# Top-k attention into a SwiGLU block: scores and V of two units in every second turn

## The chip, the cores and the metric

The kernel runs on one core of one Trainium2 chip. Its engines run side by side, each with its own in-order queue: TensorE (PE) multiplies matrices into PSUM, VectorE (DVE) selects, ScalarE (ACT) copies out of PSUM and takes exponentials, GpSimd (POOL) does elementwise work, SyncE (SP) issues most transfers. The metric is the device time of one execution in microseconds: a median of 1810.34 us over 8 runs before the change (1808.96 to 1812.03).

## The reference

```python
B, H, S, D = q.shape              # 8, 8, 576, 64, float32
scores = scale * np.matmul(q, k.transpose(0, 1, 3, 2))
kth = np.partition(scores, -32, axis=-1)[..., -32:-31]
scores = np.where(scores >= kth, scores, -1000000000.0)
scores = scores - np.max(scores, axis=-1, keepdims=True)
attn = np.exp(scores)
attn = attn / (np.sum(attn, axis=-1, keepdims=True) + 1e-09)
x = np.matmul(attn, v).transpose(0, 2, 1, 3).reshape(B * S, H * D)
g = x @ w_gate                    # 512 x 1536
silu = g * (1.0 / (1.0 + np.exp(-g)))
out = silu * (x @ w_val) @ w_out  # 1536 x 512
```

Each query keeps its 32 largest scores of 576. The attention's output, 4608 tokens of 512, goes through a feed-forward block (FFN).

## The kernel before

**Units and turns.** The attention is cut into 160 units, in the order of (batch, query tile, pair of heads): 8 batches, 5 query tiles (four of 128 queries, a last one of 64), 4 pairs of heads. A unit of the first four tiles holds two heads of 128 queries, 1152 columns of scores. A unit of the last tile holds 64 queries of both heads on the 128 partitions, so it counts as one head of 576 columns; a batch ends with four such units. The main loop has a turn n for each unit, and in it several units are worked on at different stages:

- DVE selects for unit n (`select`, L316): four rounds of MAX8 and, between them, MATCH_REPLACE8 on each head, then a mask (L338).
- POOL adds the mask to the scores of unit n-1 (`penalize`, L342). ACT then takes the exponential and its sum (`weigh`, L353), and DVE ends the turn with the reciprocal (L371).
- ACT multiplies by that reciprocal at the start of the next turn (`scaled`, L374), for unit n-2. PE transposes that unit in nine pieces of 128 columns (`turn`, L376), and ACT copies them to `et` (L387).
- PE multiplies V with the transposed weights of unit n-3 (`values`, L391). ACT copies the result to the FFN's input xT (L430).
- PE computes the scores of unit n+1 (`scores`, L278), and ACT copies them to `sc` (L313).
- `fetch` prepares unit n+2: at a batch's first query tile it transposes q and k (`prep`, L248), at the last one it loads q and k of the next batch (`load`, L213).

**Shapes on PE.** The array of 128 rows and 128 columns is used in three shapes. FFN and transposes use all of it. In the scores each of two heads contracts over 64 rows, so two matmuls run side by side in row halves (64*128 in the profile). In V's product each head gives 64 columns, so two run side by side in column halves (128*64). V's last 64 keys of both heads are multiplied at once before the others, on the whole array, with a block-diagonal matrix `vl` of V (L406). The four chunks of other keys follow in column halves (L415). An fp32 matmul is two instructions in the profile.

**The FFN in between.** The FFN goes by blocks of 256 tokens (`feed`, L456), once all four pairs of heads have written their columns of xT. It is a generator: each step, a *piece*, is 8 PE instructions of 256 columns (cost 1) or 6 (cost 0.75, in the second product, which is done with seven half-size products). Two pieces make one gate product or one value product, in one of three PSUM buffers. ACT then works on it: three instructions for a gate (L495 to L497), one copy for a value (L502). These wait in the list `on_act` until `flush(on_act)` is called, at the start of a turn and after the next two pieces, or when `piece` finds two waiting. POOL's products wait in `on_pool` likewise. `share(n)` gives each turn a credit of pieces, about 4.4 for a unit of two heads, from which the cost of the attention's work on PE in that turn is taken.

**Buffers.** Scores, transposes, V's product and the preparation share five PSUM buffers in turn (`ps_t`). `sc` and `e` have three buffers each and `et` two. MATCH_REPLACE8 of unit n+1 writes the `e` buffer that the transposes of unit n-2 read.

**Order.** Every engine but SP executes in the order in which the code issues its instructions: the last lines chain them so. SP's queue is in order too. In turn n PE has V of unit n-3, scores of n+1, two pieces, transposes of n-2, then the other pieces. ACT has what `on_act` holds, `scaled`, the copy to xT, the score copies, `weigh`, `on_act` again, the copies to `et`.

Of the kernel before, what the change touches and what calls it, by code (L numbers as in the profile page):

```python
# [10 lines left out]
FP32 = mybir.dt.float32  # L11
# [4 lines left out]
P = 128  # L16
# [4 lines left out]
BLK = 256  # L21
# [4 lines left out]
def kernel(  # L26
# [37 lines left out]
    nc = tc.nc  # L64
    B, H, S, D = q.shape
    DM, DFF = w_gate.shape
    J = S // P
    JP = J * P
    R = S - JP
    NHP = H // 2  # L70
# [15 lines left out]
    ps_t = ctx.enter_context(tc.tile_pool(name="ps_t", bufs=5, space=PSUM))  # L86
# [6 lines left out]
    for i in range(NV):  # L93
        vt = consts.tile([P, P], FP32, name=f"vlast{i}")
# [135 lines left out]
    vs = {}  # L230

    def load_v(i):
        b, hp = pairs[i]
        h = slice(2 * hp, 2 * hp + 2)
        vt = slabs.tile([P, 2, J, D], FP32, tag="v", name="v")
        v_last = slabs.tile([R, 2, D], FP32, tag="vl", name="v_last")
        vl = vlast[i % NV]
        nc.sync.dma_start(
            vt[:].rearrange("p h j d -> p h (j d)"),
            v[b, h, 0:JP].rearrange("h (p j) d -> p h (j d)", j=J),  # L240
        )
        nc.sync.dma_start(v_last[:], v[b, h, JP:S].rearrange("h p d -> p h d"))
        for hh in range(2):
            o = hh * R
            nc.sync.dma_start(vl[o : o + R, o : o + R], v[b, 2 * hp + hh, JP:S])
        vs[i] = (vt, v_last, vl)
# [24 lines left out]
    units = [(b, qt, hp) for b in range(B) for qt in range(J + 1) for hp in range(NHP)]  # L271
    state = {}

    def n_heads(qt):

        return 1 if qt == J else 2

    def scores(n):  # L278
        b, qt, hp = units[n]
        slab = preps[b * NHP + hp]  # L280
        sc = work.tile([P, 2 * S], FP32, tag="sc", name="sc", bufs=3)
        halves = [slice(0, D), slice(D, P)]
        half = S // 2

        def bank():
            return ps_t.tile([P, 512], FP32, tag="t", name="s")


        if qt == J:
            banks = [bank() for _ in range(2)]  # L290
            for i, ps in enumerate(banks):
                for d in halves:
                    k0 = R + i * half
                    nc.tensor.matmul(  # L294
                        ps[d, 0:half], slab[d, S + R : S + 2 * R], slab[d, k0 : k0 + half]
                    )
            yield
            for i, ps in enumerate(banks):
                nc.scalar.copy(sc[:, i * half : (i + 1) * half], ps[:, 0:half])
        else:  # L300
            q0 = S + 2 * R + qt * P
            banks = []
            for i in range(2):
                for hh, d in enumerate(halves):
                    ps = bank()
                    banks.append((i + 2 * hh, ps))
                    k0 = (1 - hh) * R + i * half
                    nc.tensor.matmul(  # L308
                        ps[:, 0:half], slab[d, q0 : q0 + P], slab[d, k0 : k0 + half]
                    )  # L310
            yield
            for i, ps in banks:
                nc.scalar.copy(sc[:, i * half : (i + 1) * half], ps[:, 0:half])  # L313
        state[n] = dict(sc=sc)
# [38 lines left out]
    def weigh(n):  # L353

        st = state[n]
        e, heads, bias = st["e"], st["heads"], st.pop("bias")
        tot = small.tile([P, 2], FP32, tag="tot", name="tot")
        for t, hs in enumerate(heads):
            nc.scalar.activation(  # L359
                e[:, hs], e[:, hs], AF.Exp, bias=bias[:, t : t + 1], scale=scale,  # L360
                accum_out=tot[:, t : t + 1],
            )
        nh = len(heads)
        nc.scalar.activation(tot[:, 0:nh], tot[:, 0:nh], AF.Identity, bias=eps[:])
        st["tot"] = tot
# [28 lines left out]

    xT, done = {}, {}

    def values(n):

        b, qt, hp = units[n]
        vt, v_last, vl = vs[b * NHP + hp]  # L400
        et = state.pop(n)["et"]
        last = qt == J
        ql = R if last else P
        av = ps_t.tile([P, P], FP32, tag="t", name="av")
        if not last:
            nc.tensor.matmul(av[:], vl[:], et[:, J, :], start=True, stop=False)  # L406
        for c in range(J + 1 if last else J):
            kl = R if c == J else P
            for hh in range(2):
                moving = (  # L410
                    et[0:kl, c, hh * R : (hh + 1) * R]
                    if last
                    else et[:, c + hh * (J + 1), :]
                )
                nc.tensor.matmul(  # L415
                    av[hh * R : (hh + 1) * R, 0:ql],
                    v_last[:, hh, :] if c == J else vt[:, hh, c, :],
                    moving,
                    start=last and c == 0,
                    stop=c == (J if last else J - 1),  # L420
                )
        c0 = b * S + qt * P
        at = c0
        while at < c0 + ql:
            kb = at // BLK
            n_c = min((kb + 1) * BLK, c0 + ql) - at
            if kb not in xT:
                xT[kb] = ffn.tile([P, NHP, BLK], FP32, tag="xT", name="xT", bufs=3)
                done[kb] = 0
            nc.scalar.copy(  # L430
                xT[kb][:, hp, at - kb * BLK : at - kb * BLK + n_c],
                av[:, at - c0 : at - c0 + n_c],
            )
            done[kb] += n_c
            at += n_c

    def store(o, g0, cols=slice(0, DM), queues=(nc.sync,)):
# [14 lines left out]
    def flush(queue):  # L452
        while queue:
            queue.pop(0)()
# [201 lines left out]
    NU = len(units)  # L656
# [22 lines left out]
    def fetch(n):  # L679

        b, qt, hp = units[n]
        i = b * NHP + hp
        if qt == 0:
            yield from prep(i)
        if qt == J and i + NHP < len(pairs):
            load(i + NHP)

    def share(n):


        others = 0.0
        for m, cost in ((n + 1, 0.7), (n - TURN, 0.6), (n - VALUES, 0.7)):
            if m >= 0:
                others += cost * (0.5 if units[m][1] == J else 1)
        if units[n + 2][1] == 0:
            others += 0.6

        beside = 6.4 if T[1] else 7.0
        return beside * n_heads(units[n][1]) / 2 - others

    def pieces(n):
        for _ in range(n):
            if credit[0] >= 1:
                credit[0] -= piece()

    def run(steps):
        for _ in steps:
            pass

    def finish_unit(n):  # L710
        values(n)
        b, qt, hp = units[n]
        if qt == J and b + 1 < B:
            load_v((b + 1) * NHP + hp)

    load(0)
    rounding(2)
# [2 lines left out]
    run(scores(0))  # L720
    early[0]()
    run(fetch(1))
    credit = [0.0]
    no = iter(())
    scaled = no
    TURN, VALUES = 2, 3
    due = [2.0]
    for n in range(NU + VALUES):
        nh = n_heads(units[n][1]) if n < NU else 1
        topk = select(n) if n < NU else no  # L730
        norm = normalize(n - 1) if 0 <= n - 1 < NU else no
        nxt = scores(n + 1) if n + 1 < NU else no
        ahead = fetch(n + 2) if n + 2 < NU else no

        def dve(k, beside=True):

            for _ in range(k * nh):
                next(topk, None)
                due[0] += 5 / 6 if beside else 0
                if due[0] >= 1:  # L740
                    due[0] -= 1
                    rounding(1)

        if n >= NU - NHP:
            credit[0] = 8.0
        else:
            credit[0] = min(credit[0] + share(n), share(n) + 1)
        flush(on_act)
        if 0 <= n - 1 < NU:
            penalize(n - 1)  # L750
        flush(on_pool)
        run(scaled)
        if n >= VALUES:
            finish_unit(n - VALUES)
        run(nxt)
        early[0]()
        if 0 <= n - 1 < NU:
            weigh(n - 1)


        dve(2, beside=False)
        if 2 <= n + 2 < NHP:
            load(n + 2)
        if n < NHP:
            load_v(n)
        pieces(2)
        flush(on_act)
        dve(1)
        dve(1)
        if 0 <= n - TURN < NU:  # L770
            run(turn(n - TURN))

        flush(on_pool)
        next(ahead, None)
        pieces(1)
        next(ahead, None)
        dve(1)
        pieces(1)
        dve(2, beside=False)
        run(topk)  # L780
        next(norm, None)
        scaled = norm
        pieces(6)
# [50 lines left out]
```

## Time and profile before

| | us |
|---|---|
| median of 8 runs | 1810.34 |
| the profiled execution's own time | 1809.62 |
| its span, first to last instruction | 1807.6 |
| PE busy | 1704.9 |
| DVE busy | 1615.5 |
| ACT busy | 1221.8 |
| POOL busy | 1039.9 |

The mean granted clock of PE is 0.963. The profile page divides the span into 40 slices of 45 us, and a digit is an engine's busy share of a slice in tenths. A busy PE in it is not PE at its peak, since matmuls are pipelined: the distance between the starts of two of them is what one costs. A line of waits names who waited and for whom, the total, how many times and the longest. A line of the timeline gives start, length, engine, line of the kernel, operation, output and inputs, shape on the array, sizes and how many instructions were merged.

### The profile page before, as it was taken

How to read it: one execution, taken by the hardware profiler on the slowest of the kernel's cores; microseconds unless marked ns; L12 is line 12 of the kernel's file. 1: busy time of each engine (PE TensorE's matmuls, PEld its weight loads, DVE VectorE, ACT ScalarE, POOL GpSimd, SP SyncE). 2: the span in 40 equal slices, each digit the busy share in tenths (PEclk: the TensorE clock that was granted, in tenths of full speed). 3: DMA queues.
4: the chain of work that ended last, by engine and by line, in shares of the span. 5: the costliest groups of instructions: out<-in, count | busy, mean ns of one | idle time of the engine just before them, and what ended most of it. 6: DMA issues, size and time to landing. Idle time of an engine off the chain costs nothing.

```text
span 1807.6 us, 30379 instructions
## 1 busy us (share of the span) xinstructions
PE 1704.9 (94%) x10756; PEld 1403.4 (78%) x10756; DVE 1615.5 (89%) x3372; ACT 1221.8 (68%) x2977; POOL 1039.9 (58%) x930
## 2 busy tenths in 40 slices
PE   4559999899999999999999999999999999999999
PEld 2437678687888778887888878888888878888877
DVE  7999999999999999998999989998999979999400
ACT  6779676676767676767666676766776667676532
POOL 5778665455564646564555546655556544646434
PEclk6559999899999999999999999999999999999989
DMA  7433030001200030001200021000300011000000
GB/s 191 127 105 94 21 86 1 13 2 45 50 12 3 14 78 5 13 1 29 67 13 1 14 62 32 1 13 4 92 1 13 1 41 28 13 1 13 1 12 12
DMA packets 109304, 59.64 MB, mean 33 GB/s; under 512 B 88544, under 2 KB 96992, under 8 KB 109152
## 3 DMA queue, kind: packets, MB, share of 16 engines
q1 hardware_dynamic: 108016, 57.37, 12.3%
q8 instruction: 85, 1.39, 0.3%
q14 instruction: 67, 0.55, 0.1%
q10 hardware_dynamic: 1136, 0.33, 0.1%
HBM read 48.23 MB, written 9.44 MB: 32 GB/s over the span
## 4 chain that ended last, share of the span: by engine, by line
PE 83%; DVE 7%; ACT 7%; POOL 2%; issue 0%; DMA 0%; SPq 0%; ACTq 0%; POOLq 0%
PE f L470 40%; PE x_ps L556 9%; PE av L415 8%; PE s L308 7%; PE y_ps L556 7%; PE etps L386 6%; DVE m L328 3%; DVE e L332 3%; PE s L294 2%; PE av L406 2%; ACT et L387 1%; PE o_ps L516 1%; ACT e L359 1%; DVE e L338 1%; DVE size L121 1%; ACT kqT L268 1%
## 5 line engine op out<-in xcount | busy, mean ns | idle before, releaser
L328 DVE MAX8 m<-e 128x8 f32<-128x576 f32 x864 | 613.8, 745 | 3.3
L350 POOL TENSOR_TENSOR e<-e,sc 128x1152 f32<-128x1152 f32 (+1 forms) x160 | 382.9, 2393 | 83.9 <-DVE tot L371 66.6
L332 DVE MATCH_REPLACE8 e<-m,e 128x576 f32<-128x576 f32 x576 | 422.9, 739 | 0.0
L470 PE MATMUL f<-xT,wg 128*128 128x256 f32 x1728 | 407.4, 384 | 0.3 <-ACT xT L430 0.3
L470 PE MATMUL f<-xT,wv 128*128 128x256 f32 x1728 | 403.4, 382 | 0.0
L470 PEld LDWEIGHTS f<-xT,wg 128*128 128x128 f32 x1728 | 322.3, 191 | 60.9 <-issue 19.8
L470 PEld LDWEIGHTS f<-xT,wv 128*128 128x128 f32 x1728 | 320.6, 190 | 59.3 <-issue 19.7
L498 POOL TENSOR_TENSOR h<-h,half_g 128x512 f32<-128x512 f32 x108 | 137.8, 1276 | 286.6 <-ACT h L497 269.0
L503 POOL TENSOR_TENSOR h<-h,val 128x512 f32<-128x512 f32 x108 | 139.7, 1293 | 189.4 <-ACT val L502 189.2
L359 ACT ACTIVATE e<-e,bias 128x576 f32<-128x576 f32 x288 | 224.8, 796 | 26.7 <-POOL e L350 26.5
L374 ACT ACTIVATE e<-e,tot 128x576 f32<-128x576 f32 x288 | 210.1, 776 | 26.2 <-DVE tot L371 26.0
L387 ACT COPY et<-etps 128x512 f32<-128x512 f32 (+1 forms) x448 | 182.5, 480 | 53.4 <-PE etps L386 52.6
L332 DVE MATCH_REPLACE8 e<-m,sc 128x576 f32<-128x576 f32 x288 | 211.4, 739 | 0.0
L328 DVE MAX8 m<-sc 128x8 f32<-128x576 f32 x288 | 202.4, 738 | 9.6 <-ACT sc L313 9.6
L386 PE MATMUL etps<-ident,e 128*128 128x128 f32 (+1 forms) x1312 | 175.8, 279 | 18.1 <-ACT xT L430 12.5
L386 PEld LDWEIGHTS etps<-ident,e 128*128 128x128 f32 (+1 forms) x1312 | 155.9, 144 | 42.6 <-issue 25.2
L313 ACT COPY sc<-s 128x288 f32<-128x288 f32 x512 | 167.6, 417 | 26.7 <-PE s L308 25.7
L308 PE MATMUL s<-kqT 64*128 64x288 f32 x1024 | 171.0, 455 | 14.1 <-ACT kqT L268 13.3
L338 DVE TENSOR_SCALAR e<-sc,m 128x576 f32<-128x576 f32 x288 | 179.2, 658 | 1.1
L415 PE MATMUL av<-et,v 128*64 128x128 f32 (+1 forms) x2560 | 172.6, 279 | 6.9 <-ACT et L387 6.9
L415 PEld LDWEIGHTS av<-et,v 128*64 128x64 f32 x2560 | 135.6, 143 | 32.0 <-ACT et L387 9.3
L495 ACT ACTIVATE h<-f 128x512 f32<-128x512 f32 x108 | 64.1, 594 | 128.1 <-PE f L470 128.1
(73 smaller groups left out, 2040.9 us busy)
## 6 DMA issues: line engine op xcount, KB each, us to landing
v<-in_v_dram SPq DMA_DIRECT2D x32, 256.0 KB, 3.0
kq_in<-in_k_dram SPq DMA_DIRECT2D x63, 128.0 KB, 2.8
kq_in<-in_q_dram SPq DMA_DIRECT2D x63, 128.0 KB, 3.0
w<-in_moe_w_gate_dram SPq DMA_DIRECT2D x12, 512.0 KB, 3.8
w<-in_moe_w_val_dram SPq DMA_DIRECT2D x12, 512.0 KB, 3.8
w<-in_moe_w_out_dram SPq DMA_DIRECT2D x12, 512.0 KB, 3.6
out_dram<-o SPq DMA_DIRECT2D x38, 128.0 KB, 2.4
out_dram<-o SPq DMA_DIRECT2D x16, 256.0 KB, 2.4
```

The lines of the kernel that those rows point to most:

```text
L308: nc.tensor.matmul(ps[:, 0:half], slab[d, q0 : q0 + P], slab[d, k0 : k0 + half])
L328: nc.vector.max(m[:, t, 8 * r : 8 * r + 8], cur[:, hs])
L332: nc.vector.match_replace(e[:, hs], m[:, t, 8 * r : 8 * r + 8], cur[:, hs], LOWEST)
L338: nc.vector.tensor_scalar(e[:, hs], sc[:, hs], m[:, t, TOP_K - 1 : TOP_K], FAR, ALU.is_lt, ALU.mult)
L350: nc.gpsimd.tensor_tensor(e[:, every], e[:, every], sc[:, every], ALU.add)
L359: nc.scalar.activation(e[:, hs], e[:, hs], AF.Exp, bias=bias[:, t : t + 1], scale=scale, accum_out=tot[:, t : t + 1],)
L374: nc.scalar.mul(e[:, hs], e[:, hs], tot[:, t : t + 1])
L386: nc.tensor.transpose(ps[0:kl, c * P : (c + 1) * P], e[:, k0 : k0 + kl], ident[:])
L387: nc.scalar.copy(et[0:kl, c0 : c0 + cn, :], ps[0:kl, 0 : cn * P].rearrange("p (c j) -> p c j", c=cn),)
L415: nc.tensor.matmul(av[hh * R : (hh + 1) * R, 0:ql], v_last[:, hh, :] if c == J else vt[:, hh, c, :], moving, start=last and c == 0, stop=c ...
L470: nc.tensor.matmul(ps[:, i, :], w[:, kc, m * P : (m + 1) * P], x[:, kc, :], start=(kc == 0), stop=(kc == KC - 1),)
L556: nc.tensor.matmul(ps, lhsT, T[i][m], start=m == 0, stop=m == MQ - 1)
```

## The change

`values` takes a list of units, and the turns differ by parity. In an even turn PE has the scores of unit n+1, V of units n-4 and n-3, and the scores of n+2. In an odd turn it has neither scores nor V, and the transposes come after one piece instead of two. The first two turns have one set of scores each. V's last keys are multiplied in column halves of `vl`, as the other keys are. Both V results lie in one PSUM buffer and go to xT in one copy (two where a block of 256 tokens ends inside the tile). On ACT of an even turn, the score copies of n+1 and the copy to xT stand ahead of `scaled`; the score copies of n+2 stand after `weigh`. On ACT of an odd turn, the copies to `et` stand ahead of `weigh`. Preparations and loads of q and k are issued one turn earlier, and `share` is adapted. Credits become about 3 in even turns and 6 in odd ones.

```diff
-    def values(n):
+    def values(ns):
...
-        av = ps_t.tile([P, P], FP32, tag="t", name="av")
-        if not last:
-            nc.tensor.matmul(av[:], vl[:], et[:, J, :], start=True, stop=False)
...
+        av = ps_t.tile([P, 2, P], FP32, tag="t", name="av")
+        for i, n in enumerate(ns):
+            assert units[n] == (b, qt, hp0 + i)
+            vt, v_last, vl = vs[b * NHP + hp0 + i]
+            et = state.pop(n)["et"]
+            for c in (*range(J), J) if last else (J, *range(J)):
+                kl = R if last and c == J else P
+                for hh in range(2):
+                    d = slice(hh * R, (hh + 1) * R)
+                    if c == J:
+                        weights_, at = (v_last[:, hh, :], d) if last else (vl[:, d], None)
+                    else:
+                        weights_, at = vt[:, hh, c, :], d if last else None
...
+                    nc.tensor.matmul(
+                        av[d, i, 0:ql],
+                        weights_,
+                        moving,
+                        start=c == (0 if last else J),
+                        stop=c == (J if last else J - 1),
+                    )
...
             nc.scalar.copy(
-                xT[kb][:, hp, at - kb * BLK : at - kb * BLK + n_c],
-                av[:, at - c0 : at - c0 + n_c],
+                xT[kb][:, hps, at - kb * BLK : at - kb * BLK + n_c],
+                av[:, 0 : len(ns), at - c0 : at - c0 + n_c],
             )
...
-        for m, cost in ((n + 1, 0.7), (n - TURN, 0.6), (n - VALUES, 0.7)):
+        costs = [(m, 0.7) for m in scored(n) + valued(n)] + [(n - TURN, 0.6)]
+        for m, cost in costs:
...
-        if units[n + 2][1] == 0:
+        if units[n + 3][1] == 0:
             others += 0.6
...
+    def scored(n):
+
+        ahead = [n + 1] if n < 2 else [] if n % 2 else [n + 1, n + 2]
+        return [m for m in ahead if m < NU]
+
+    def valued(n):
+
+        behind = [] if n % 2 else [n - 4, n - 3]
+        return [m for m in behind if 0 <= m < NU]
...
     run(fetch(1))
+    load(2)
...
-        nxt = scores(n + 1) if n + 1 < NU else no
-        ahead = fetch(n + 2) if n + 2 < NU else no
+        nxt = [scores(m) for m in scored(n)]
+        ahead = fetch(n + 3 if n else 2) if n + 3 < NU else no
...
         flush(on_pool)
+        if nxt:
+            run(nxt.pop(0))
+        if valued(n):
+            finish_units(valued(n))
+        if nxt:
+            next(nxt[0])
         run(scaled)
-        if n >= VALUES:
-            finish_unit(n - VALUES)
-        run(nxt)
+        flipped = turn(n - TURN) if 0 <= n - TURN < NU else no
+        if n % 2:
+            pieces(1)
+            run(flipped)
         early[0]()
         if 0 <= n - 1 < NU:
             weigh(n - 1)
+        if nxt:
+            run(nxt.pop())
...
-        if 2 <= n + 2 < NHP:
-            load(n + 2)
+        if n == 0:
+            run(ahead)
+            load(3)
+            ahead = fetch(3)
...
-        if 0 <= n - TURN < NU:
-            run(turn(n - TURN))
+        run(flipped)
```

More of the change, by code (lines that the diff above doesn't have):

```diff
@@ L395 @@
     xT, done = {}, {}
-    def values(n):
-        b, qt, hp = units[n]
-        vt, v_last, vl = vs[b * NHP + hp]
-        et = state.pop(n)["et"]
+    def values(ns):
+        b, qt, hp0 = units[ns[0]]
         last = qt == J
         ql = R if last else P
-        av = ps_t.tile([P, P], FP32, tag="t", name="av")
-        if not last:
[L406 to L421, printed above, removed]
+        av = ps_t.tile([P, 2, P], FP32, tag="t", name="av")
[11 more added lines that the diff above has]
+                        weights_, at = vt[:, hh, c, :], d if last else None
+                    moving = (
+                        et[0:kl, c, at]
+                        if last
+                        else et[:, c + (0 if c == J else hh * (J + 1)), :]
+                    )
[5 more added lines that the diff above has]
+                        stop=c == (J if last else J - 1),
+                    )
         c0 = b * S + qt * P
         at = c0
+        hps = slice(hp0, hp0 + len(ns))
         while at < c0 + ql:
@@ L430, in values @@
             nc.scalar.copy(
-                xT[kb][:, hp, at - kb * BLK : at - kb * BLK + n_c],
-                av[:, at - c0 : at - c0 + n_c],
+                xT[kb][:, hps, at - kb * BLK : at - kb * BLK + n_c],
+                av[:, 0 : len(ns), at - c0 : at - c0 + n_c],
             )
-            done[kb] += n_c
+            done[kb] += n_c * len(ns)
             at += n_c
@@ L708, in run, with finish_units @@
             pass
[L710 to L714, printed above, removed]
+    def finish_units(ns):
+        values(ns)
+        for n in ns:
+            b, qt, hp = units[n]
+            if qt == J and b + 1 < B:
+                load_v((b + 1) * NHP + hp)
     load(0)
@@ L725 @@
     scaled = no
-    TURN, VALUES = 2, 3
+    TURN = 2
     due = [2.0]
-    for n in range(NU + VALUES):
+    for n in range(NU + 3):
         nh = n_heads(units[n][1]) if n < NU else 1
```

## The prediction

> **What bounds the kernel now.** I read the page's first two parts, then the list of waits by TensorE (PE) and by VectorE (DVE), then the order of time of one steady turn on PE and on ScalarE (ACT). From the page:
>
> ```profile
> span 1807.6 us, 30379 instructions
> PE 1704.9 (94%) x10756; PEld 1403.4 (78%) x10756; DVE 1615.5 (89%) x3372; ACT 1221.8 (68%) x2977; POOL 1039.9 (58%) x930
> ...
> PE   4559999899999999999999999999999999999999
> ...
> DVE  7999999999999999998999989998999979999400
> ```
>
> PE is full from the fifth slice (about 200 us) to the end, DVE from the second slice to 1700 us. So two engines are near their limit, and the stage decides. The waits say which:
>
> ```profile
> PE av L406 <- ACT et L387: 52.3, 27, 5.7
> ```
>
> ```profile
> DVE tot L371 <- ACT tot L364: 78.8, 31, 14.4
> ...
> DVE e L332 <- PE etps L386: 25.1, 29, 2.3
> ```
>
> The columns are microseconds, times, longest. Most of PE's 52.3 us lie before 200 us and at the end. I took the start of every turn (a unit's first MAX8 on DVE, its first transpose on PE) from the trace and summed over the 20 turns of one batch. Batches 2 to 6 (turns 40 to 139, 441 to 1487 us) last 207 to 212 us, with 1 to 4 us of idle PE and 7 to 13 us of idle DVE; DVE alone would need 199 to 201. Here PE's work is the length. In batches 0 and 1 (to 441 us) DVE sets the pace: in batch 1 DVE idles 4.4 us and PE 8.0. After 1700 us only PE works.
>
> One turn on PE (start, length, instructions; an fp32 matmul is recorded as two):
>
> ```profile
> 913.85 3.62 PE L470 MATMUL f<-xT,wg 128*128 128x256 f32 x16
> ...
> 917.30 0.38 PE L406 MATMUL av<-et,vlast 128*128 128x128 f32 x2
> ...
> 917.62 1.09 PE L415 MATMUL av<-et,v 128*64 128x128 f32 x16
> ...
> 918.64 1.24 PE L308 MATMUL s<-kqT 64*128 64x288 f32 x8
> ...
> 919.81 3.72 PE L470 MATMUL f<-xT,wv 128*128 128x256 f32 x16
> ...
> 923.37 1.15 PE L386 MATMUL etps<-ident,e 128*128 128x128 f32 x9
> ```
>
> The reader is to see the array's three shapes: whole (128*128), column halves (128*64), row halves (64*128). Nothing waits here, yet start minus start is more than the work. The trace's single starts give the running rate: whole, 0.109 us at 128 columns and 0.216 at 256; a pair of column halves, both together, 0.109; a pair of row halves at 288 columns, 0.242. Against these rates the first two instructions after each change of shape come late: into columns 0.096 + 0.051 = 0.147 us; into rows 0.100 + 0.105 = 0.205; into the whole array 0.097 + 0.104 = 0.201. Sum 0.553 per unit, and the same from the groups: L415 took 1.02 for 8 x 0.109 = 0.87, L308 1.17 for 4 x 0.242 = 0.97, the next L470 3.56 for 16 x 0.216 = 3.46.
>
> **The change part by part.** *Shapes on PE.* Two units now cost six changes (whole, columns, rows, twice): 1.106 us. Afterwards an even turn goes whole, rows, columns, rows, whole and an odd turn stays whole: 2 x 0.205 + 0.147 + 0.201 = 0.758. Saved: 0.35 us per two units. Whole to rows and rows to columns do not occur without a wait before. Bounds: nothing for either gives 1.106 - 0.406 = 0.70 saved, 0.205 for both gives 0.29. I price by the shape entered, since the first delay was 0.096 to 0.100 in all three and the second differs with the new shape's weights. It counts where PE is the length: batches 2 to 7, 60 pairs of units, and two pairs of the end: 62 x 0.35 = 21.7 us (18 to 43).
>
> The trace has a first delay of 0.096 to 0.100 and a second of 0.051 to 0.105 at each change it shows, and is silent on the two that are new. [...]
>
> *Last keys in column pairs.* Two whole instructions at 0.109 become two rounds of column halves at 0.109: nothing, between a loss of 0.05 and a gain of 0.05 per unit (3 us in all).
>
> *One copy for both V results.* 192 copies of 0.242 us (L430) become 96. Some 10 to 20 us of ACT, but ACT is 68% busy, and idle 102.1 us just before these copies waiting for PE. Nothing; if that cover were gone, at most 20 us gained.
>
> *What moves on ACT.* One turn of it:
>
> ```profile
> 917.50 0.60 ACT L495 ACTIVATE h<-f 128x512 f32<-128x512 f32 x1 [2.87 <-PE f L470]
> 918.00 0.59 ACT L496 ACTIVATE half_g<-f 128x512 f32<-128x512 f32 x1
> 918.47 0.63 ACT L497 ACTIVATE h<-h 128x512 f32<-128x512 f32 x1
> 918.99 1.44 ACT L374 ACTIVATE e<-e,tot 128x576 f32<-128x576 f32 x2
> 920.33 0.26 ACT L430 COPY xT<-av 128x128 f32<-128x128 f32 x1
> 920.47 1.31 ACT L313 COPY sc<-s 128x288 f32<-128x288 f32 x4
> 921.64 0.82 ACT L359 ACTIVATE e<-e,bias 128x576 f32<-128x576 f32 x1
> ```
>
> By starts: gate 1.49, normalization 1.34, four score copies 1.17, the two exp with their total 1.93, three et copies 1.10, value copy 0.48. ACT begins 0.20 after PE would start its next instruction (917.30 and 917.50).
>
> Even turn, from its start on PE: scores to 1.16, both V to 3.48, second scores to 4.64, two FFN pieces to 8.29, transposes to 9.27, one piece to 11.0. ACT waits for V to 3.68, copies to 3.93, normalizes to 5.27, exp to 7.2, second score copies to 8.37. The second scores need the banks of the first, copied by about 3.3 at the latest, before PE gets there at 3.48; the transposes need them at 8.73, free from 7.6. No wait on PE. Behind ACT's new wait for V stand the normalization, exp and DVE's reciprocal (L371): done at 7.25 instead of 6.3. DVE's free turn is 10.56, so PE may trail DVE by 3.3 us instead of 4.4 before DVE waits. That costs nothing while PE is full.
>
> Odd turn: PE does one piece (1.73 us), then the transposes, which need the normalization, which stands behind what ACT still holds of the FFN. Where the even turn's last piece finishes a gate product: gate from 0.20 to 1.69, first head normalized at 2.45, second at 3.13, each 0.05 more to reach PE; PE is there at 1.73 and, for the second head, 0.44 later. It loses 0.8 + 0.2 = 1.0 us. In the instruction order this stands in six odd turns past turn 36 (63, 67, 69, 89, 95, 115): 6 us. A small copy before a 1.30 us piece costs 0.4, in eight turns: 3 us. In the others the normalization is in time.
>
> *One-head turns* (four at each batch's end). Walked with the same durations, the even turn's chain (V, normalization, exp, score copies, et copies, next normalization at 9.6) meets PE at 9.2 where that turn has one piece, at 7.6 where it has none. Idle PE: 1.9 us for batches 3 and 4, 3 to 4 for 1, 2, 5, 6; together 18 against 15.6 before. Loss 2.4, between a gain of 5 and a loss of 20.
>
> *Start and SP's queue.* Load(2) stands before the weights' first transfers past the start, load(3) and a third preparation in turn 0. DVE is full from 11 us on and its first scores stay ahead of them: nothing; were scores for unit 2 late by a load (2.8 to 3.0 us each), 3 us. The loads of later batches are issued one turn earlier and keep their distance to the preparations that free their buffers. POOL's queue keeps its order within a turn. The FFN pieces by turn 156 are 558.5 of 622.5 in both orders, the tail 34.5 in both, so work is not moved past DVE's end.
>
> Sum: -21.7 + 6 + 3 + 2.4 = -10.3. The profiled execution has a span of 1807.6 and took 1809.62, 0.7 under the median of 1810.34. 1809.6 - 10.3 = 1799.3; on the median's scale 1800.
>
> **The rivals.** *A, ACT's queue takes the place (slower).* PE waits for the normalization not in six odd turns but in most. For it: by the durations above (8.8 pieces of FFN counted) ACT is busy 15.4 of 22 us per two turns, and now waits for V first; POOL's penalty (2.6 us, L350) stands before exp. Against: without a gate ahead the normalization ends near PE's arrival. Of the 60 odd turns in batches 2 to 7, 54 are counted above without a gate ahead. At 1.0 us each, 10 further turns undo the gain, from 14 on it is slower (1814), 26 give 1826, all 54 give 1854.
>
> *B, break-even.* One-head turns cost 12 us more than before instead of 2.4, by waits that are longer than walked: 1800 + 9.6 = 1810, within 3.6.
>
> *C, no new wait at all, or shapes cheaper than priced.* 1810.3 - 21.7 = 1788.6; with the 0.70 of the upper bound 1767. DVE's 199 us per batch would allow 6 x 10 = 60 us, so DVE doesn't stop it.
>
> *D, PE wasn't the length.* If DVE paced batches 2 to 7, nothing would come: 1810. Against: no PE idle in their two-head turns save 0.4 and 0.7 us.
>
> **How the numbers follow.** This kernel's measurement tells 0.2% (3.6 us). Forecast, 1793 to 1806.7: 0.40. C, below 1793: 0.18. B and D, within 3.6 us: 0.16. A: 0.26. So faster 0.58, same 0.16, slower 0.26. The low end is 1786 (C's full saving and a little of its bound; about 0.08 lies below), the high end 1826 (A at 26 further turns; about 0.12 lies above).
>
> **What would show it.** PE's busy time and idle in the two-head turns of batches 2 to 6: the batch at about 207 instead of 209 us. In the timeline of an even turn, rows, columns, rows with delays of 0.205, 0.147, 0.205. Waits of PE etps for ACT e (L374, 0.5 us now) of some 10 us in odd turns. Waits of DVE tot for ACT tot stay or shrink. Wrong, if PE etps waits on ACT sum above 30 us, if V or scores wait for ACT's copies in even turns, or if DVE's idle time grows while PE's does.

## The result, and the profile after

The changed kernel takes 1820.66 us, a median of 10 runs (1818.0 to 1824.11), against 1810.33 us for the kernel before, run beside it (28 runs, 1808.8 to 1812.73). The ratio is 1.0057, with a 95% interval of 1.0049 to 1.0065. It is slower by 0.6%, or 10.3 us; 1800 us and a gain were forecast, so the direction was wrong. The profiled execution has a span of 1819.9 us, 12.3 more than before.

Here are the page's totals and its 40 slices for PE and DVE:

```profile
span 1819.9 us, 30839 instructions
PE 1692.3 (93%) x11012; PEld 1388.7 (76%) x11012; DVE 1629.2 (90%) x3372; ACT 1210.8 (67%) x2881; POOL 1041.5 (57%) x930
...
PE   5448999799999999999999999999999999999999
...
DVE  7999899999999989998999989998999989999300
```

PE's busy time is 12.6 us shorter than before, and yet the span is longer. A 7 now stands in PE's eighth slice (318 to 364 us) instead of an 8, and DVE's last mask ends 13.5 us later (1729.9 us instead of 1716.4). The lists of waits of PE and DVE over the whole run begin so (who waited for whom, us, times, longest; PE's three longest, DVE's longest):

```profile
PE etps L386 <- ACT e L374: 47.2, 17, 7.1
PE etps L386 <- ACT sc L313: 23.4, 17, 3.5
PE s L308 <- ACT sc L313: 20.2, 6, 6.2
```

```profile
DVE tot L371 <- ACT tot L364: 86.1, 26, 12.2
```

The transposes' wait for the normalization, 0.5 us before, is 47.2 us. That looks like the rival of ACT's queue with its most expensive reading, but 40.3 us of it lie before 450 us, where DVE sets the pace. After 450 us PE's list is this:

```profile
PE etps L386 <- issue: 6.1, 6, 2.2
PE etps L386 <- ACT sc L313: 5.2, 7, 1.4
PE etps L386 <- ACT e L374: 3.3, 5, 0.7
PE x_ps L562 <- POOL h L610: 3.0, 2, 1.6
PE etps L386 <- POOL bias L348: 2.1, 1, 2.1
PE etps L386 <- POOL e L350: 0.7, 1, 0.7
PE x_ps L562 <- POOL h L577: 0.5, 1, 0.5
```

A list that names the last event puts one cause under several names here: "issue", "POOL bias" and "POOL e" stand for the same wait of L386, for an ACT that is late: in each of these, ACT ends a normalization (L374) 0.10 to 0.14 us before PE goes on.

Where the 12.3 us came from, by DVE's first MAX8 of a unit (its first turn, turn 20, turn 40, turn 140) and its last instruction: turns 0 to 19 are 7.8 us longer (235.8 instead of 228.0, with a beginning 0.4 earlier), batch 1 is 4.5 longer (206.1 instead of 201.6), batches 2 to 6 together are 0.1 longer, batch 7 and the end 0.3. So the stage for which the whole gain was forecast gained nothing, and the start, priced at nothing, lost the time.

For the steady stage I added up PE's starts from the transposes of turn 40 (they are of unit 38) to those of turn 140: the work at the running rates, the delays of the first two instructions after a change of shape, and what is left as waits, time at half clock included (shown below).

| us | before | after | odd turns' transposes late (below) |
|---|---|---|---|
| work at the running rates | 970.4 | 969.8 | 971.0 |
| delays at changes of shape | 56.3 | 42.2 | 42.4 |
| waits | 20.0 | 37.1 | 22.7 |
| length (the parts within 0.6) | 1047.3 | 1049.5 | 1035.8 |

The gain at the shapes is there: 14.1 us. New waits took 17.1. One even turn of PE in the changed kernel (start, length, line, instructions):

```profile
704.31 3.62 PE L476 MATMUL f<-xT,wv 128*128 128x256 f32 x16
707.86 1.24 PE L308 MATMUL s<-kqT 64*128 64x288 f32 x8
709.03 0.44 PE L420 MATMUL av<-et,vlast 128*64 128x128 f32 x4
...
711.36 1.24 PE L308 MATMUL s<-kqT 64*128 64x288 f32 x8
712.53 2.86 PE L562 MATMUL y_ps<-wo,h 128*128 128x256 f32 x12
```

Scores 1.17, both V 2.33, scores 1.17, with four changes of shape instead of six per two units and no wait among them: this is what the prediction walked through.

### The profile page after: what moved, and what is told of

The parts are those of the page before. It is cut to its first block, busy times and chain, and to the rows that moved or that the text cites. A ratio compares the mean times of both kernels' runs of the same rounds, so it can differ in the third digit from the quotient of the medians.

```text
span 1819.9 us, 30839 instructions
## 1 busy us (share of the span) xinstructions
PE 1692.3 (93%) x11012; PEld 1388.7 (76%) x11012; DVE 1629.2 (90%) x3372; ACT 1210.8 (67%) x2881; POOL 1041.5 (57%) x930
## 4 chain that ended last, share of the span: by engine, by line
PE 76%; DVE 11%; ACT 7%; POOL 4%; issue 2%; DMA 1%; SPq 0%; ACTq 0%; POOLq 0%
PE f L476 37%; PE x_ps L562 9%; PE av L420 8%; PE etps L386 7%; PE s L308 6%; PE y_ps L562 5%; DVE m L328 5%; DVE e L332 4%; PE s L294 2%; ACT e L359 1%; ACT e L374 1%; DVE e L338 1%; PE kqps L263 1%; PE o_ps L522 1%; POOL e L350 1%
## 5 line engine op out<-in xcount | busy, mean ns | idle before, releaser
L332 DVE MATCH_REPLACE8 e<-m,e 128x576 f32<-128x576 f32 x576 | 423.0, 740 | 0.0
L476 PE MATMUL f<-xT,wg 128*128 128x256 f32 x1728 | 402.8, 382 | 0.0
L386 PE MATMUL etps<-ident,e 128*128 128x128 f32 (+1 forms) x1312 | 191.4, 286 | 83.2 <-ACT e L374 47.2
L386 PEld LDWEIGHTS etps<-ident,e 128*128 128x128 f32 (+1 forms) x1312 | 154.8, 145 | 128.5 <-POOL e L350 37.1
L387 ACT COPY et<-etps 128x512 f32<-128x512 f32 (+1 forms) x448 | 186.2, 488 | 88.1 <-PE etps L386 84.6
L359 ACT ACTIVATE e<-e,bias 128x576 f32<-128x576 f32 x288 | 221.0, 772 | 17.7 <-POOL e L350 17.7
L374 ACT ACTIVATE e<-e,tot 128x576 f32<-128x576 f32 x288 | 211.2, 784 | 10.4 <-DVE tot L371 10.4
L332 DVE MATCH_REPLACE8 e<-m,sc 128x576 f32<-128x576 f32 x288 | 211.5, 739 | 0.0
L338 DVE TENSOR_SCALAR e<-sc,m 128x576 f32<-128x576 f32 x288 | 193.6, 708 | 1.1
L420 PE MATMUL av<-et,v 128*64 128x128 f32 (+1 forms) x2560 | 158.1, 267 | 0.0
L308 PEld LDWEIGHTS s<-kqT 64*128 64x128 f32 x1024 | 97.9, 197 | 73.1 <-issue 25.9
```

The source lines that it names most:

```text
L308: nc.tensor.matmul(ps[:, 0:half], slab[d, q0 : q0 + P], slab[d, k0 : k0 + half])
L332: nc.vector.match_replace(e[:, hs], m[:, t, 8 * r : 8 * r + 8], cur[:, hs], LOWEST)
L338: nc.vector.tensor_scalar(e[:, hs], sc[:, hs], m[:, t, TOP_K - 1 : TOP_K], FAR, ALU.is_lt, ALU.mult)
L359: nc.scalar.activation(e[:, hs], e[:, hs], AF.Exp, bias=bias[:, t : t + 1], scale=scale, accum_out=tot[:, t : t + 1],)
L374: nc.scalar.mul(e[:, hs], e[:, hs], tot[:, t : t + 1])
L386: nc.tensor.transpose(ps[0:kl, c * P : (c + 1) * P], e[:, k0 : k0 + kl], ident[:])
```

## The experiments

Each kernel below was timed beside the kernel before (1810.35 us for the first four, 1810.71 for the last four). The edits are to the changed kernel unless said otherwise.

**1. The old start.** Turns 0 to 15 in the old order, the loads of q and k in the old places.

```diff
-        ahead = [n + 1] if n < 2 else [] if n % 2 else [n + 1, n + 2]
+        ahead = [n + 1] if n < N0 else [] if n % 2 else [n + 1, n + 2]
...
-        behind = [] if n % 2 else [n - 4, n - 3]
+        behind = [n - 3] if n <= N0 else [] if n % 2 else [n - 4, n - 3]
...
-    load(2)
...
+    TURN, N0 = 2, 16
...
-        ahead = fetch(n + 3 if n else 2) if n + 3 < NU else no
+        ahead = fetch(n + (2 if n < 4 else 3)) if n + 3 < NU else no
...
-        if nxt:
+        if n < N0:
+            run(scaled)
+        elif nxt:
             run(nxt.pop(0))
...
-        if nxt:
+        if n < N0:
+            run(nxt.pop())
+        elif nxt:
             next(nxt[0])
...
-        if n % 2:
+        if n % 2 and n >= N0:
...
-        if n == 0:
-            run(ahead)
-            load(3)
-            ahead = fetch(3)
+        if 2 <= n + 2 < NHP:
+            load(n + 2)
```

> The changed kernel, but turns 0 to 15 in the order of before (one unit's V and scores in every turn, normalization first, transposes after two pieces, loads and preparations at their old places). Turn 20 starts on VectorE at 239.1 us before and at 246.4 after, turn 40 at 440.7 and 452.5; the sixteenth turn after holds a wait of VectorE for the exp of 6.3 us, which PE's late transposes (2.5 and 3.7 us of idle in turns 11 and 13, then 1.6 us each at half clock) have pushed ahead. Theory (the start loses it): 7 to 9 us less than the changed kernel, 1812 to 1814, and no such wait in turn 16. Rival (a loss spread over all turns that the start only shows first): within 3 us of the changed kernel, 1818 to 1823.

Measured: 1813.98 us, 1.0018 [1.0009, 1.0027] of the time before, 6.7 less than the changed kernel. Turn 20 begins at 238.6 us on DVE (239.1 before, 246.4 after the change). So the start's loss comes from the order of the first 16 turns, loads and preparations included, and goes with it; which of these parts costs what, this run does not separate. What DVE waits for in the changed kernel's first 250 us, where before only the first MAX8 and the first memory fill waited:

```profile
DVE m L328 <- ACT sc L313: 9.2, 1, 9.2
DVE tot L371 <- ACT tot L364: 6.3, 1, 6.3
DVE size L121 <- ACT size L114: 3.0, 2, 2.2
```

The 6.3 us stand at turn 16. In the turns before it ACT still rounds the weights, so the normalization is late, and the odd turns' transposes with it:

```profile
177.20 1.89 PE L476 MATMUL f<-xT,wv 128*128 128x256 f32 x8
182.83 1.41 PE L386 MATMUL etps<-ident,e 128*128 128x128 f32 x9 [3.74 <-ACT e L374]
184.03 3.54 PE L476 MATMUL f<-xT,wv 128*128 128x256 f32 x8
```

```profile
178.69 0.74 ACT L114 ACTIVATE size<-w 128x512 f32<-128x512 f32 x1
...
179.83 0.71 ACT L117 ACTIVATE w<-w 128x512 f32<-128x512 f32 x1
180.38 0.64 ACT L501 ACTIVATE h<-f 128x512 f32<-128x512 f32 x1
...
181.86 1.49 ACT L374 ACTIVATE e<-e,tot 128x576 f32<-128x576 f32 x2
```

L114 to L117 round a piece of the weights, and a gate's three instructions follow; only then does the normalization (L374) begin. PE stands 3.74 us, since in its queue the transposes are ahead of the pieces that could run. The 3.0 us at L121 are in turn 0, where the third preparation and its loads have moved in front.

**2. The odd turns' transposes late.** They stay after two pieces, at the place they had, in all turns; on ACT the copies to `et` are then behind exp again.

```diff
-        if n % 2:
-            pieces(1)
-            run(flipped)
         early[0]()
```

> The changed kernel, but an odd turn does its transposes after two pieces, behind the exp on ScalarE, as an even one. From turn 40 on PE waits 24 us at the transposes of odd turns, a further 3 us pass at half clock behind the two waits over 2 us, and the start has 6.2 us of waits and 3.2 us at half clock of the same kind. Theory (the early transposes of odd turns meet the normalization): these waits go, PE saves some 30 us, VectorE allows about 200 us per batch, so 1792 to 1804. Rival (what bounds is the shorter slack between PE and VectorE, or VectorE's own slower mask): PE's waits move to VectorE, 1812 to 1822.

Measured: 1797.08 us, 0.9925 [0.9913, 0.9937]: 23.6 less than the changed kernel and faster than the kernel before by 0.75%. By the same starts on DVE, 4.0 of the 23.3 us of span come from the time up to turn 20, 5.4 from batch 1, 13.3 from batches 2 to 6. The waits of 6.3 and 3.0 us that DVE has in the start are down to 1.4 and 1.9. The delays at the shapes are unchanged (table above), the waits are down from 37.1 to 22.7. PE's waits of this kernel from 440 to 1480 us begin so:

```profile
PE etps L386 <- ACT sc L313: 5.0, 6, 1.5
PE kqps L263 <- ACT et L387: 3.3, 3, 1.7
PE x_ps L562 <- POOL h L610: 2.3, 3, 1.6
PE x_ps L562 <- POOL xT L569: 1.7, 1, 1.7
```

The waits under "issue" and "POOL bias" are down to 0.9 and 1.1 us, those under "ACT e" are gone; the preparation's wait of 3.3 us for the copies to `et` is new. Without this one part, three lines, the change gains. The edit moves PE's transposes and ACT's copies together; which of the two counts, it does not tell.

**3. Odd turns normalize ahead of the gate.** The transposes stay early, but ACT does their normalization before what it still holds of the FFN.

```diff
+        if n % 2:
+            run(scaled)
         flush(on_act)
```

> The changed kernel, but in odd turns ScalarE normalizes before it works off what it holds of the FFN. Theory (a fresh gate product ahead of the normalization holds PE's transposes): the six waits of 0.88 + 0.2 us in turns 63, 67, 69, 89, 95, 115 go, and the small ones behind a copy, 6 to 9 us in all: 1811 to 1815. Rival (the normalization is late for other reasons, its reciprocal or the turn before): within 3 us of 1820.7.

Measured: 1813.01 us, 1.0015 [1.0006, 1.0023], 7.7 less than the changed kernel. From turn 40 to 140 PE's waits at L386 fall from 27.6 to 19.7 us, by 7.8; the waits at turns 63, 67, 69, 89, 95 and 115 are gone. This is the six gates and the small copies, priced at 6 + 3. In the profiled executions, which lie 11.3 us apart, turns 0 to 19 are 3.5 us shorter as well, so the median's 7.7 is not these waits alone. The whole is a third of what the early transposes cost.

**4. Even turns normalize ahead of score copies and V's copy.** The last of the four things that the change does, undone.

```diff
         flush(on_pool)
+        run(scaled)
         if nxt:
             run(nxt.pop(0))
...
-        run(scaled)
```

> The changed kernel, but in even turns ScalarE normalizes ahead of the score copies and of V's copy, as before: the last part of the change alone is undone. My prediction priced that part at nothing. Theory (it is nothing while PE is full): within 4 us of 1820.7; the second scores then wait for the copies of the first by up to 0.7 us in turns that start with a gate product. Rival (V's wait ahead of the normalization is what costs): 1810 or less.

Measured: 1812.62 us, 1.0015 [1.0006, 1.0023]: 8.0 less. My theory had priced this at nothing and it falls here; the rival's 1810 was not reached either. In the transposes from turn 40 to 140 the waits at L386 fall by 8.4 us (27.6 to 19.2), 7.3 of it in the one-head turns: the wait ahead of the fifth transpose, which needs the bank of the second score copies, is 0.25 to 0.26 us instead of 0.87 to 0.88 in turns 58, 78 and 98, and at the first transpose turn 57 waits 0.96 instead of 1.96 and turns 77 and 97 no longer (0.51). A turn of one head has so little other work on PE that what stands ahead of the normalization on ACT is not hidden. Batch 1 goes the other way: it is 2.1 us longer than in the changed kernel, 208.2.

**5. The kernel before, with only the last keys in column pairs.**

```diff
-            nc.tensor.matmul(av[:], vl[:], et[:, J, :], start=True, stop=False)
+            for hh in range(2):
+                d = slice(hh * R, (hh + 1) * R)
+                nc.tensor.matmul(av[d, :], vl[:, d], et[:, J, :], start=True, stop=False)
```

> The kernel before with one part of the change alone: V's last keys in column halves, two rounds of 0.109 us in place of two whole instructions of 0.109, and the array enters columns one product earlier. Theory (the prediction's term of nothing): within 3 us of 1810.4. Rival (column halves cost or save something by themselves): 128 units at 0.05 us, 6 us to either side.

Measured: 1809.15 us, 0.9992 [0.9984, 1.0001]. Nothing that can be told from no change, as priced.

**6. Late transposes, with one copy to xT per unit.** Number 2, and the joint copy undone.

```diff
-            nc.scalar.copy(
-                xT[kb][:, hps, at - kb * BLK : at - kb * BLK + n_c],
-                av[:, 0 : len(ns), at - c0 : at - c0 + n_c],
-            )
+            for i in range(len(ns)):
+                nc.scalar.copy(
+                    xT[kb][:, hp0 + i, at - kb * BLK : at - kb * BLK + n_c],
+                    av[:, i, at - c0 : at - c0 + n_c],
+                )
```

> The run with the late transposes (1797.1 us), with V's two results copied to xT one by one, 96 copies more. Theory (the prediction: ScalarE waits for PE ahead of these copies, their number is nothing): 1795 to 1801. Rival (the copy now stands ahead of the normalization, so each further one delays exp and the second scores' banks by 0.14 us and more): 1802 to 1808.

Measured: 1801.14 us, 0.9945 [0.9933, 0.9958], 4.1 more than number 2 by the medians and 1.8 more by the spans of the profiled executions (1798.4 and 1796.6). The intervals overlap and the value lies at the border of what the two theories expected. The joint copy may be worth 2 to 4 us; these runs do not settle it.

**7. Late transposes, and even turns normalize ahead.** Numbers 2 and 4 together.

```diff
         flush(on_pool)
+        run(scaled)
...
-        run(scaled)
         flipped = turn(n - TURN) if 0 <= n - TURN < NU else no
-        if n % 2:
-            pieces(1)
-            run(flipped)
```

> Two undone at once: transposes of odd turns after two pieces, and the normalization ahead of the score copies and V's copy in even turns. Alone they gave 23.6 and 8.0 us less than the changed kernel. Theory 1 (the early normalization helped only because the early transposes of odd turns waited behind ScalarE's whole chain): nothing is left for it, 1795 to 1800. Theory 2 (waiting for V ahead of the normalization costs by itself, at the transposes of even turns, 6 us of waits for score copies, and through POOL at the FFN's second product, 6 us): 1787 to 1793.

Measured: 1794.49 us, 0.9908 [0.9894, 0.9921], 2.6 less than number 2. The value lies between what the two theories expected, and the intervals of numbers 2 and 7 overlap. The traces say more. From turn 40 to 140 PE takes 1030.5 us instead of 1035.8 with number 2, 5.3 less, where number 4 alone took 9.5 off the changed kernel; turn 40 begins 2.4 us later on DVE (445.5 instead of 443.1), which takes part of that back. The two costs are thus in part the same wait: turn 57's at the first transpose, 1.96 us in the changed kernel, goes with late transposes alone. In part they are not: ahead of the fifth transpose, turns 58, 78, 98, 118 and 138 still wait 0.87 to 0.88 us in number 2, and 0.25 to 0.32 here.

**8. The same, with the old start.** Numbers 1, 2 and 4 together; the edits of number 1 to `scored`, `valued` and the loads, and in the loop:

```diff
         run(scaled)
-        if nxt:
+        if n >= N0 and nxt:
             run(nxt.pop(0))
...
-        if nxt:
+        if n < N0:
+            run(nxt.pop())
+        elif nxt:
             next(nxt[0])
```

> The run before this one, with turns 0 to 15 in the order of before as well. With late transposes turn 20 starts at 242.4 us on VectorE, before the change at 239.1; alone, the old start gave 6.7 us less. Theory (the start's loss that the late transposes leave): 3 us less than the run before this one. Rival (it was the same waits, now gone): within 1.5 us of it.

Measured: 1789.72 us, 0.9885 [0.9872, 0.9899], the fastest of all, and 4.8 less than number 7 where 3 were expected. It beats the kernel before by 1.15% and the changed kernel by 31 us. The page's totals and slices for PE:

```profile
span 1786.3 us, 30803 instructions
PE 1687.1 (94%) x11012; PEld 1395.6 (78%) x11012; DVE 1619.3 (91%) x3372; ACT 1206.3 (68%) x2888; POOL 1044.9 (58%) x930
...
PE   4549999799999999999999999999999999999999
```

Turn 20 begins at 238.8 us, batches 2 to 6 last 203.5 to 208.7 instead of 207.2 to 212.2 (batch 2 to 6 before: 209.3, 208.3, 209.1, 207.2, 212.2).

## Why the prediction was wrong, step by step

Forecast were 10.3 us less, and the span of the profiled execution grew by 12.3. Of the 22.6 between them about 7 stand in the start, 4 in batch 1, 7 in batches 2 to 6 and 4 in batch 7 and the end.

**Right: shapes on PE.** Six changes were priced at 1.106 us per two units, four at 0.758, with two kinds of change that no row had shown. In the starts of the changed kernel whole to rows has a first delay of 0.093 us and rows to columns of 0.096, with the second delay going with the shape entered (0.10 and 0.05): 0.35 us saved per pair of units. The lower and the upper bound of the price (0.29 and 0.70) are out. The size was off by a little: 14.1 us from turn 40 to 140 where 50 pairs at 0.35 make 17.5. The pairs of one-head units save nearly nothing, since their last keys pass through a fourth shape (64*64 in the profile), which the sum of the prediction did not have, and so keep seven changes of eight. By these delays a change costs 0.15 us into columns and 0.20 into the others. What in PE takes this time, no run shows; that the second delay differs with the weights is my reading of three numbers (0.051, 0.105 and 0.104 us).

**Right: odd turns with a gate ahead, one-head turns.** The six turns named wait 0.84 to 0.88 us at the first transpose and about 0.2 more at the later ones. One of them, with its PE and its ACT rows:

```profile
742.07 1.89 PE L476 MATMUL f<-xT,wv 128*128 128x256 f32 x8
744.68 1.34 PE L386 MATMUL etps<-ident,e 128*128 128x128 f32 x9 [0.72 <-ACT e L374]
```

```profile
742.27 0.60 ACT L501 ACTIVATE h<-f 128x512 f32<-128x512 f32 x1 [1.97 <-PE f L476]
742.76 0.59 ACT L502 ACTIVATE half_g<-f 128x512 f32<-128x512 f32 x1
743.24 0.63 ACT L503 ACTIVATE h<-h 128x512 f32<-128x512 f32 x1
743.76 1.44 ACT L374 ACTIVATE e<-e,tot 128x576 f32<-128x576 f32 x2
```

The normalization stands behind the gate's three instructions and PE stands 0.72 us. In the list the wait is shorter by 0.15 than by starts, since a matmul's recorded length (0.38 us at 256 columns) reaches past its successor's start (0.22 us after its own). Experiment 3 took 7.8 us of such waits away where 9 were priced. The one-head turns of batches 2 to 6 hold 17.1 us of waits of the transposes after the change; the walk gave 18 for six, some 14.4 for these five (twice 1.9 and three times 3.55). So in the steady stage the two waits that I named have about the sizes that I gave them. What I didn't ask is what the early place of the transposes gives in return. It is little: DVE, which waits for them at L332, waits 12.3 us in all with early ones and 14.9 with late ones, and experiment 2 is 23.6 us faster with the late ones.

**Wrong: "Start and SP's queue", priced at nothing.** This is the largest single miss: turn 20 begins 7.3 us late, and experiment 1 ends 6.7 us earlier. The step followed the loads and DVE's first scores, and didn't walk ACT's and PE's order through turns 1 to 16, where ACT has the weights to round besides, and PE is not full. The words "DVE is full from 11 us on" were taken as cover; they hold as long as nobody makes DVE wait, and the waits of 6.3 and 3.0 us above are such waits.

**Wrong: the sum counted batches 2 to 7 only.** Batch 1 was left out of the gain, rightly, since DVE sets its pace, but, save for its one-head turns, also out of the loss. It is 4.5 us longer. From the transposes of turn 20 to those of turn 40 PE's waits are 21.6 us instead of 14.2 (at the transposes 16.4 instead of 2.7); with late transposes they are 16.3, and the batch is back at 200.7 us. But PE's waits count here only as far as they reach DVE, and DVE's own show 1.6 us of the 4.5: 5.8 instead of 4.2 (at L371 and L332). DVE's busy time grew by 2.6 us (196.4 to 199.0), nearly all of it in the mask (19.9 to 22.4 us in this batch, 20.3 with late transposes, and 27.4 in experiment 4). So more than half of the batch's loss is the slower mask of the next section, a cost that no step of the prediction had. A stage in which a change gains nothing can still lose.

**Wrong: "Behind ACT's new wait for V ... That costs nothing while PE is full."** Experiment 4 measures 8.0 us for it in the changed kernel and experiment 7 2.6 us with late transposes. The clause "while PE is full" is what failed: it isn't full in the one-head turns, where 7.3 us of the waits that experiment 4 took away stood. I had walked the one-head turns as part of the whole change, and not asked which part of the wait each edit made.

**Smaller: "One copy for both V results. ... Nothing".** By experiment 6 it may be worth 2 to 4 us; that it is not nothing isn't shown. The bound of 3 us for the last keys should have been 6 (128 units at 0.05); nothing rested on it, and experiment 5 shows no change.

**Left out: FFN's second product.** L562 waits for POOL in turns 55, 101, 102, 109 and 127, 4.3 us in all from turn 40 to 140 by the starts, 0.6 before. The step said that "POOL's queue keeps its order within a turn"; but PE's pieces have moved between the turns (3 and 6 instead of 4.4), and so probably reach POOL's results sooner; no run tested this. And the clock, below, 1.7 us. In batch 7 and the end 12 pairs at 0.35 should have saved 4.2 us, and they took 0.3 more; from 1500 to 1700 us PE's waits at L562 are 2.2 us instead of 0.7, and the rest of this miss stays open.

**The balance of the steady stage**, turn 40 to 140: forecast 17.5 saved, 9 and about 2 lost, 6 to 7 gained; measured 2.2 lost on PE's starts (0.1 by DVE's). The shapes fell short by 3.4, the second product took 3.7 more, the clock 1.7: together 8.8, and 8.7 lie between a gain of 6.5 and a loss of 2.2.

**The rivals.** The side is that of rival A, but not by its mechanism: it wanted waits for the normalization in 14 or more further odd turns of batches 2 to 7 at 1.0 us each. Such waits came in few further two-head turns (0.7 us at turn 101, 0.3 and less at other odd ones). Mostly the loss is outside of these batches, where no rival stood. The sign that the prediction named for being wrong, waits of the transposes on ACT above 30 us, came (47.2), but most of it before 450 us. Rival B's place, the one-head turns, is where the order on ACT cost, but the turns as a whole waited about as walked. C needed no new wait and is out. D is out: batches 2 to 6 got shorter where PE's waits went, in experiments 2 and 8, and DVE's own limit (199 to 201 us a batch) was not reached.

## What the runs showed of the hardware

**One wait, two clocks.** A wait of 2.23 us ahead of the same transposes, in the changed kernel and in experiment 3 (PE's rows of turn 117):

```profile
1268.45 1.68 PE L386 MATMUL etps<-ident,e 128*128 128x128 f32 x9 [2.23 <-issue]
1269.92 2.77 PE L562 MATMUL y_ps<-wo,h 128*128 128x256 f32 x6
1272.48 1.63 PE L562 MATMUL x_ps<-t,xT 128*128 128x256 f32 x6
1273.94 0.60 PE L263 MATMUL kqps<-ident,kq_in 128*128 128x128 f32 x4
```

```profile
1258.91 1.39 PE L386 MATMUL etps<-ident,e 128*128 128x128 f32 x9 [2.23 <-POOL bias L348]
1260.13 1.46 PE L562 MATMUL y_ps<-wo,h 128*128 128x256 f32 x6
1261.43 1.46 PE L562 MATMUL x_ps<-t,xT 128*128 128x256 f32 x6
1262.72 0.60 PE L263 MATMUL kqps<-ident,kq_in 128*128 128x128 f32 x4
```

In the first, six instructions take 2.56 us from start to start, in the second 1.30. By windows of 4 us the granted clock is 0.62 in the one and 1.00 in the other (start and end, length, PE's busy time, clock, share of DMA, GB/s; first the changed kernel, then experiment 3):

```profile
1268.45:1272.40 3.95, 3.95 (x15) 0.62 0.00 0
```

```profile
1258.90:1262.90 4.00, 3.99 (x23) 1.00 0.00 0
```

In the first, one instruction of L562 stands 0.427 us from the next, in the second 0.216: half the rate. From the first transpose to the preparation (L263) PE takes 5.49 us in the one and 3.81 in the other, so behind this wait the lower clock cost 1.7 us on top. From 440 to 1500 us, in windows of 4 us, such a clock (0.62 to 0.74 in the lowest window) shows once in the kernel before (after a wait of 2.73 us at 1465 us), twice in the changed one (2.23 and 2.13), once in experiment 3 (2.12), twice in experiment 1 (1.80 and 2.13), once in experiment 7, and not at all in experiments 2, 4, 5, 6 and 8. Waits of 1.80 and 2.23 us occur with and without it: 1.80 in experiment 1 with a clock of 0.62 (636 to 640 us) and in the changed kernel, in turn 57, with 1.00 (644 to 648 us); 2.23 as shown above. What decides, no run here shows.

**The mask on DVE beside POOL.** The mask's instruction (L338, 128x576) takes 0.51 us in its median and up to 2.96. Over the run its time was 179.2 us before and 193.6 after. The 172 of 288 that begin while no elementwise instruction of POOL runs take 506 ns in the mean after the change, the other 116 take 1007 (before: 175 at 506 and 113 at 893). What in the two engines makes a mask longer that begins beside POOL, no run here shows. Why the 116 cost more after the change than the 113 before (the excess over the median is 42.6 us before, 57.0 after, 40.3 in experiment 2, 63.0 in experiment 4) was not tested and stays open. Where PE is the length it need not reach the time, but in batch 1, where DVE sets the pace, it did: 2.5 of 4.5 us.

## What to carry to other kernels

Price every stage for a loss, not only the stage that gains: here the steady batches came out near zero, and the start and the batch in which another engine sets the pace lost 12 us, a part of it in that engine's own instructions and not in any wait. When a change moves several things at once, ask of each move what waits for it at its new place; moving the transposes earlier gained little and put PE's queue behind ACT, and undoing it made a loss of 0.6% into a gain of 0.75%. A cover such as "while PE is full" has to be checked turn by turn, and it ends where the turns are short.
